# Issuing one group's load of x three bundles later in a fused convolution and channel-mix kernel

## The chip, the cores and the metric

The kernel runs on one core of one Trainium2 chip. The metric is the device time of one launch in microseconds. Before the change it is 434.34 us, the median of three runs (433.48, 434.34 and 434.85). The profile is of one further execution, with a span of 432.2 us.

The engines of a core are named as in the profile: PE is TensorE (PEld its weight loads), DVE is VectorE, ACT is ScalarE, POOL is GpSimd, SP is SyncE. SP and POOL start transfers here: SP those of the convolution's result and of the output, POOL those of x.

## The reference

There are 8 sequences of 4160 rows with 192 channels. The first half is a causal convolution over 7 rows, with 8 heads of 24 channels and softmaxed weights; the second half mixes each row with the one before it and sends it through a gated two-layer network.

```python
# weight: (8, 7), softmaxed over its last axis -> w
out = np.einsum('hk,bskhg->bshg', w, x_unf)     # 7 rows back, per head; called y below

x_prev = shift(y, 1)                            # the row before, zeros at the start
xk = mu_k * y + (1.0 - mu_k) * x_prev           # = x_prev + mu_k * (y - x_prev)
xr = mu_r * y + (1.0 - mu_r) * x_prev
k = np.maximum(xk @ w_k, 0.0)                   # 192 -> 1024
v = k * k @ w_v                                 # 1024 -> 192
r = 1.0 / (1.0 + np.exp(-(xr @ w_r)))
return (r * v).astype(np.float32)
```

(Shortened: `shift` stands for a concatenation with zeros.)

## The kernel before

The sequences are taken in four pairs. Work is cut into **steps** of 512 rows of a pair, and emitted in **bundles** of four k-slots; a full step has 8 slots, so two bundles. The first pair has steps of 256, 7 times 512 and 256 rows and fills bundles 0 to 15; the second pair's first step begins at bundle 16.

Ahead of the steps runs the convolution, in **groups** of up to ten blocks of 120 rows. There are six groups for the first pair (numbers 0 to 5) and four for each other pair (6 to 9 for the second, and so on). A group goes through these stages:

- `load_x`: POOL loads x for both sequences of the pair into a buffer `xb` of a ring of three, from f32 in memory to bf16 in the buffer. A full group is two transfers of 480 KB.
- `conv_half`, `conv_out`: PE multiplies `xb` with a banded matrix `toe`, in four units; ACT copies the result to `y`.
- `y_write`: SP writes `y` to memory (`y_dram`).
- `y_read`: SP reads it back transposed into `yT`, channels on partitions. (Groups 1 to 3 are transposed on PE instead, group 0 in a way of its own.)

A step then takes the difference of neighbouring rows from `yT` (`diff`), and makes xk and xr of it on DVE (`scale`, `add_y`). These feed the k and r matmuls.

```python
three = ctx.enter_context(tc.tile_pool(name="three", bufs=3))
...
def x_tile(g):
    p, blk0, nb, _, _ = groups[g]
    xb = three.tile([P, GB, 2, D], BF16, tag="xb", name="xb")
    xbs[g] = xb
    if g > 4:
        nc.vector.memset(xb[0:1, 0, 0, 0:2], 0.0)
    ...

def load_x(g):
    ...
    for s in range(2):
        ...
        nc.gpsimd.dma_start(out=xb[:, lo:hi, s, :], in_=bass.AP(...))   # the line that the profile calls L125

def y_write(g):
    ...
    nc.sync.dma_start(out=y_drams[p][blk0 * BLK : (blk0 + nb) * BLK, :]..., in_=ys[g][:BLK, :nb, :])

def y_read(g):
    ...
    nc.sync.dma_start_transpose(
        out=yTs[p][:, :, YC + r0 : YC + r1], in_=y_drams[p][r0:r1, :]
    )
```

When each stage is emitted is kept in tables by bundle. `fb` is the bundle of the first step that needs the group.

```python
for g, (p, blk0, nb, fb, on_pe) in enumerate(groups):
    ...
    elif p == 0:
        xs = {2: [0], 3: [1, 1], 4: [2, 2, 3, 3], 5: [4, 4, 5, 5]}[g]   # bundles of the conv units
    else:
        xs = range(fb - 10, fb - 10 + nx)
    ...
        at(late, xs[-1], y_write, g)
        at(late, xs[-1] + (1 if g < 6 else 2), y_read, g)
    if g > 3:
        b = {4: 1, 5: 1, 6: 2}.get(g)
        b = first_bundle[first_step[p]] + (-15, -11, -7, -3)[(g - 6) % 4] if b is None else b
        at(early, b, x_tile, g)
        at(early, b, load_x, g)
for s, (p, t0, L, n0, ns) in enumerate(steps):
    fb = first_bundle[s]
    ...
        if s == 4:
            at(mix_a, fb - 1, diff, s)
        else:
            at(mix_c, fb - 2, diff, s)
        at(mix_a, fb - 1, scale, s, 0, 0)
        at(mix_b, fb - 1, scale, s, 0, 1, 2)
        at(mix_b, fb - 1, scale, s, 1, 0)
        at(mix_c, fb - 1, add_y, s, 0)
```

For the groups that matter here this gives:

| group | rows of the pair | load issued in bundle | convolution in bundles | y_write | y_read | first needed by |
|---|---|---|---|---|---|---|
| 4 | 1920 to 3119 of pair 0 | 1 | 2, 2, 3, 3 | 3 | 4 | diff of step 4, in bundle 6 |
| 5 | 3120 to the end of pair 0 | 1 | 4, 4, 5, 5 | 5 | 6 | diff of step 6, in bundle 9 |
| 6 | 0 to 1199 of pair 1 | 2 | 6, 7, 8, 9 | 9 | 11 | first step of pair 1, bundle 16 |
| 7 | 1200 to 2399 of pair 1 | 16 - 11 = 5 | 10, 11, 12, 13 | 13 | 15 | third step of pair 1 |
| 8 | 2400 to 3599 of pair 1 | 16 - 7 = 9 | 14 to 17 | 17 | 19 | fifth step of pair 1 |

One bundle emits its work in this order, and each engine runs its own instructions in the order of emission:

```python
def bundle_rest(b, ns):
    units = xt.get(b, []) + [None, None]
    quad = vq.get(b, [None])[0]
    for n in bundles[b - 1][2:] if b > 1 else ():
        k_square(n)                      # DVE, the last two of the bundle before
    run(mix_a, b)
    k_mm(ns[0]); k_relu(ns[0]); k_square(ns[0])      # PE, ACT, DVE
    run(mix_b, b)
    conv_half(units[0], 0)
    k_mm(ns[1])
    conv_half(units[0], 1)
    k_relu(ns[1]); k_square(ns[1])
    run(rq, b)                           # the r matmuls
    run(first, b)
    if quad: v_rows(*quad, 0)            # 32 matmuls
    conv_half(units[1], 0)
    k_mm(ns[2])
    conv_half(units[1], 1)
    k_relu(ns[2])
    if quad: v_rows(*quad, 1)            # 32 matmuls
    run(mix_c, b)
    k_mm(ns[3]); k_relu(ns[3])
    if quad: v_out(*quad)                # product on DVE, two output stores of 192 KB on SP
    run(late, b)
```

`run(early, b)` comes before this. (Several calls are put on one line here.)

Of the kernel before, what the change touches and what calls it, by code (L numbers as in the profile page):

```python
# [14 lines left out]
def kernel(  # L15
# [254 lines left out]
    def conv_units(g):  # L270

        if groups[g][2] * 4 * G <= BANK:
            return [((0, 1), (6, 7)), ((2, 3), (4, 5))]
        return [((0,), (1,)), ((3,), (4,)), ((6,), (7,)), ((2,), (5,))]
# [367 lines left out]
    def at(table, b, fn, *a):  # L642
        table.setdefault(b, []).append((fn, a))
# [11 lines left out]
    for g, (p, blk0, nb, fb, on_pe) in enumerate(groups):  # L655
        nx = 1 if g < 3 else len(conv_units(g))
        if g == 0:
            continue
        if g == 1:
            xs = []  # L660
        elif p == 0:
            xs = {2: [0], 3: [1, 1], 4: [2, 2, 3, 3], 5: [4, 4, 5, 5]}[g]
        else:
            xs = range(fb - 10, fb - 10 + nx)
        for i, b in enumerate(xs):
            if g == 2:
                at(late, b, conv, g, i)
            else:
                xt.setdefault(b, []).append((g, i))
        if on_pe:  # L670
            for j in range((nb + 3) // 4):
                at(first, g - 1, tr, g, j)
        else:
            at(late, xs[-1], y_write, g)

            at(late, xs[-1] + (1 if g < 6 else 2), y_read, g)
        if g > 3:

            b = {4: 1, 5: 1, 6: 2}.get(g)
            b = first_bundle[first_step[p]] + (-15, -11, -7, -3)[(g - 6) % 4] if b is None else b  # L680
            at(early, b, x_tile, g)
            at(early, b, load_x, g)
# [174 lines left out]
```

## Time and profile before

| what | value |
|---|---|
| time, median of three | 434.34 us |
| span of the profiled execution | 432.2 us |
| PE busy | 411.6 us, 95% |
| DVE busy | 381.4 us, 88% |
| ACT busy | 347.5 us, 80% |
| POOL busy | 48.9 us, 11% |
| moved by the DMA engines | 64.58 MB, mean 149 GB/s |
| the chain that ended last | PE 88%, DMA 5%, DVE 3% |
| in that chain, DMA into yT | 4% |

A row of the profile's timeline gives start, length, engine, the line of the kernel, the operation with its destination and source, and the number of instructions. A bracket holds the time that the engine idled before, and the instruction or transfer that ended this. For a transfer, a row of SPq or POOL is its issue; when the data has landed is told apart from that. The chain of work that ended last is followed back from the last instruction, at each step to what released it: what is not in the chain can get faster without any effect on the end. The slices cut the span into 40 equal parts, with the busy share in tenths.

### The profile page before, as it was taken

Reading aid. Unit: us, or ns where it says so; the run is one execution under the profiler, and the core shown is the slowest. Engines: PE = TensorE matmul, PEld = TensorE weight load, DVE = VectorE, ACT = ScalarE, POOL = GpSimd, SP = SyncE. Lnnn points to the kernel's source line nnn. Section 1 sums busy time; section 2 is a strip of 40 time slices with the busy share of each in tenths; the row PEclk is TensorE's granted clock in tenths of the full one; section 3 lists DMA queues with packets and bytes.
Section 4 is the critical chain, followed back from the end, with each engine's and each line's share of the span. In section 5 each row is a group of like instructions: output and inputs, shape, how many; then the busy total and the mean of one; then the engine's idle time right before and its main releaser. Section 6 shows DMA issues by size and latency. Waiting matters only on the chain.

```text
span 432.2 us, 15786 instructions
## 1 busy us (share of the span) xinstructions
PE 411.6 (95%) x6845; PEld 315.7 (73%) x6845; DVE 381.4 (88%) x678; ACT 347.5 (80%) x407; POOL 48.9 (11%) x73
## 2 busy tenths in 40 slices
PE   7799974999999999999999999999999999999995
PEld 3456752777787887787777877787777877777795
DVE  5887827899999999999999999999999999999973
ACT  4878972889888898889888888889888888777771
POOL 6550100020203010020203010020200000000000
PEclk9989995999999999999999999999999999999999
DMA  8996795395949989395849999395848573411223
GB/s 133 192 180 95 178 188 164 83 215 136 183 119 192 208 170 202 87 212 145 172 131 169 227 172 197 83 212 148 176 125 149 160 162 118 109 56 64 74 77 110
DMA packets 134502, 64.58 MB, mean 149 GB/s; under 512 B 85132, under 2 KB 134048, under 8 KB 134432
## 3 DMA queue, kind: packets, MB, share of 16 engines
q1 hardware_dynamic: 96050, 48.31, 43.9%
q0 software_dynamic: 37488, 14.66, 29.8%
q8 instruction: 53, 0.87, 0.8%
q10 hardware_dynamic: 894, 0.61, 0.5%
q14 instruction: 17, 0.14, 0.1%
HBM read 29.92 MB, written 36.99 MB: 155 GB/s over the span
## 4 chain that ended last, share of the span: by engine, by line
PE 88%; DMA 5%; DVE 3%; ACT 1%; POOL 1%; issue 1%; SPq 0%; ACTq 0%; DVEq 0%
PE ps_k L490 38%; PE ps_v L592 37%; PE ps_r L564 7%; PE ps_c L291 5%; DMA yT<-y_dram 4%; DMA wk<-in_moe_w_k_dram 2%; PE ps_v L547 1%; DVE k L533 1%; ACT k_sb L519 1%; DVE d L433 0%; DVE xk L470 0%; DVE xk L464 0%; POOL xb L125 0%; PE ps_t L380 0%; DVE yT L389 0%
## 5 line engine op out<-in xcount | busy, mean ns | idle before, releaser
L519 ACT ACTIVATE k_sb<-ps_k 128x1024 bf16<-128x1024 f32 x260 | 260.9, 1037 | 63.9 <-PE ps_k L490 63.6
L490 PE MATMUL ps_k<-xk,wk 64*128 64x512 bf16 (+1 forms) x1632 | 203.4, 370 | 10.0 <-DVE xk L470 9.5
L533 DVE TENSOR_TENSOR k<-k_sb 128x1024 bf16<-128x1024 bf16 x260 | 177.6, 688 | 15.9 <-ACT k_sb L519 8.4
L592 PE MATMUL ps_v<-wv,k 64*128 64x192 bf16 x4032 | 188.8, 243 | 0.6 <-ACT k_sb L519 0.6
L592 PEld LDWEIGHTS <-k 64*128 64x128 bf16 x4032 | 172.3, 94 | 13.2 <-issue 0.6
L490 PEld LDWEIGHTS <-wk 64*128 64x128 bf16 x1632 | 87.5, 95 | 63.7 <-DVE xk L470 10.2
L608 DVE TENSOR_TENSOR o_sb<-ps_v,r_sb 128x768 f32<-128x768 f32 x64 | 61.2, 957 | 14.0 <-PE ps_v L592 9.8
L336 ACT CAST y<-ps_c 120x960 bf16<-120x960 f32 (+4 forms) x67 | 50.9, 787 | 6.4 <-PE ps_c L291 6.4
L572 ACT ACTIVATE r_sb<-ps_r 128x768 bf16<-128x768 f32 x65 | 54.6, 840 | 0.0
L125 POOL DMA_DIRECT2D xb<-in_x_dram x34 | 30.8, 911 | 208.0 <-PE ps_c L291 140.1
L564 PEld LDWEIGHTS <-xr 64*128 64x128 bf16 x780 | 36.1, 95 | 13.3 <-DVE xb L105 2.0
L564 PE MATMUL ps_r<-wr,xr 64*128 64x192 bf16 x780 | 44.0, 243 | 1.7 <-DVE xb L105 1.7
L291 PE MATMUL ps_c<-xb,toe 64*128 64x480 bf16 (+2 forms) x240 | 40.3, 343 | 0.0
L433 DVE TENSOR_TENSOR d<-yT 128x1536 bf16<-128x1536 bf16 (+2 forms) x35 | 31.0, 887 | 8.7 <-DMA yT<-y_dram 8.6
L464 DVE TENSOR_SCALAR xr<-d,mu 128x512 bf16<-128x512 bf16 (+1 forms) x102 | 35.1, 348 | 0.0
L464 DVE TENSOR_SCALAR xk<-d,mu 128x512 bf16<-128x512 bf16 (+1 forms) x99 | 32.8, 361 | 0.1
L470 DVE TENSOR_TENSOR xr<-xr,yT 128x1536 bf16<-128x1536 bf16 (+1 forms) x33 | 31.0, 939 | 1.1
L470 DVE TENSOR_TENSOR xk<-xk,yT 128x1536 bf16<-128x1536 bf16 (+1 forms) x32 | 30.2, 942 | 0.0
L291 PEld LDWEIGHTS <-toe 64*128 64x128 bf16 x240 | 13.5, 96 | 12.4 <-issue 1.1
L417 POOL COPY y_tail<-yT 128x195 bf16<-128x195 bf16 x4 | 1.8, 453 | 68.5 <-DMA yT<-y_dram 68.5
L719 PE MATMUL warm<-zeros,ones_t 128*128 128x512 bf16 x16 | 5.6, 530 | 1.8 <-DVE zeros L734 1.8
L107 POOL MEMSET xb<- 32x384 bf16 x3 | 1.2, 408 | 45.9 <-PE ps_k L490 43.7
(54 smaller groups left out, 64.3 us busy)
## 6 DMA issues: line engine op xcount, KB each, us to landing
out_dram<-o_sb SPq DMA_DIRECT2D x128, 192.0 KB, 2.7
y_dram<-y SPq DMA_DIRECT2D x10, 900.0 KB, 6.5
xb<-in_x_dram POOLq DMA_DIRECT2D x14, 480.0 KB, 8.2
xb<-in_x_dram POOLq DMA_DIRECT2D x6, 432.0 KB, 8.2
xb<-in_x_dram POOLq DMA_DIRECT2D x10, 192.0 KB, 5.2
y_dram<-y SPq DMA_DIRECT2D x3, 450.0 KB, 5.6
y_dram<-y SPq DMA_DIRECT2D x1, 810.0 KB, 6.7
xb<-in_x_dram POOLq DMA_DIRECT2D x2, 384.0 KB, 7.4
```

Of the source, the lines that this page charges most:

```text
L291: nc.tensor.matmul(out=banks[:, bank, :, :, k * G : (k + 1) * G], lhsT=toe[q, h, :], rhs=xbs[g][q, :nb, :, h * G : (h + 1) * G], start=hal ...
L336: copy(out=bass.AP(tensor=y.tensor, offset=y.offset + d0, ap=[y.ap[0], [d1 - d0, 2], [2 * D, nb], [Q, 2], [1, n]],), in_=bass.AP(tensor=ps ...
L433: nc.vector.tensor_tensor(out=shaped(s, diffs[s][:, cs, :L]), in0=y_of(s, cs, 1), in1=y_of(s, cs, 0), op=ALU.subtract)
L464: nc.vector.tensor_scalar(out=t[:, c, :L], in0=diffs[s][:, c, :L], scalar1=mu[:, i, c : c + 1], scalar2=None, op0=ALU.mult)
L470: nc.vector.tensor_tensor(out=o, in0=o, in1=y_of(s, sl, 0), op=ALU.add)
L490: nc.tensor.matmul(out=ps[:, i, f * L : (f + 1) * L], lhsT=wk[r, c, fs], rhs=xk[r, c, :L], start=c == 0 and f == 0, stop=c == NC - 1 and f ...
L519: nc.scalar.activation(out=k_sb, in_=ps.rearrange("p a b -> p (a b)"), func=AF.Relu)
L533: nc.vector.tensor_tensor(out=o, in0=i, in1=i, op=ALU.mult)
L564: nc.tensor.matmul(out=ps[:, i, k * D : (k + 1) * D], lhsT=xr[q, c, ts], rhs=wr[q, c, :], start=c == 0, stop=c == NC - 1,)
L572: nc.scalar.activation(out=r_sbs[s, j], in_=ps[:, :, 0 : 2 * D], func=AF.Sigmoid)
L592: nc.tensor.matmul(out=v_ps[s, j][:, bank, k * D : (k + 1) * D], lhsT=k2s[s][q, f, t * P : (t + 1) * P], rhs=wv[q, f, :], start=half == 0 ...
L608: nc.vector.tensor_tensor(out=o_sb.rearrange("p (b t) d -> p b (t d)", b=2), in0=v_ps.pop((s, j)), in1=r_sbs.pop((s, j)), op=ALU.mult,)
```

## The change

Only the bundle changes in which group 7's buffer is taken and its load is issued: 8 instead of 5. Its convolution stays in bundles 10 to 13. The change is meant to keep this load from running beside transfers of the first pair that are wanted sooner.

```diff
@@ -676,7 +676,7 @@
             at(late, xs[-1] + (1 if g < 6 else 2), y_read, g)
         if g > 3:
 
-            b = {4: 1, 5: 1, 6: 2}.get(g)
+            b = {4: 1, 5: 1, 6: 2, 7: 8}.get(g)
             b = first_bundle[first_step[p]] + (-15, -11, -7, -3)[(g - 6) % 4] if b is None else b
             at(early, b, x_tile, g)
             at(early, b, load_x, g)
```

## The prediction

> **What bounds the kernel now.** I read the page's slices first, then the chain of work that ended last, then the timeline around the one hole that the chain shows, then the same kind of transfer elsewhere in the trace. The slices (each 432.2 / 40 = 10.8 us):
>
> ```profile
> PE   7799974999999999999999999999999999999995
> ...
> PEclk9989995999999999999999999999999999999999
> ```
>
> TensorE is busy at nine tenths or more from slice 7 to slice 38, at the full clock. After the start-up there is one weak place: slices 5 and 6 (54 to 76 us), where PE falls to 7 and 4 tenths and its clock to half in slice 6. The chain of waits names it (start, length, what):
>
> ```profile
> 50.42 15.70 DMA yT<-y_dram
> 66.15 0.97 DVE d L433
> 70.42 1.46 PE ps_k L490 x6
> ```
>
> Everywhere after this the chain is PE work end to end. So for 15.7 us the end of the kernel hangs on one transposed read, the y_read of group 4 (the fifth group). The timeline shows what is issued beside it and who waits (start, length, engine, line, operation; in brackets the idle time before and its releaser):
>
> ```profile
> 49.97 1.88 POOL L125 DMA_DIRECT2D xb<-in_x_dram  x2 [19.57 <-PE ps_c L291]
> ...
> 50.42 10.82 SPq L367 DMA_TRANSPOSE yT<-y_dram  x1
> ...
> 57.79 1.50 PE L592 MATMUL ps_v<-wv,k 64*128 64x192 bf16 x32
> ...
> 61.07 0.83 PE L490 MATMUL ps_k<-xk,wk 64*128 64x512 bf16 x6
> ...
> 66.15 0.96 DVE L433 TENSOR_TENSOR d<-yT 128x1536 bf16<-128x1536 bf16 x1 [8.60 <-DMA yT<-y_dram]
> ...
> 70.42 1.46 PE L490 MATMUL ps_k<-xk,wk 64*128 64x512 bf16 x6 [8.52 <-DVE xk L470]
> ...
> 74.47 1.48 PE L592 MATMUL ps_v<-wv,k 64*128 64x192 bf16 x32
> ...
> 80.60 1.49 PE L592 MATMUL ps_v<-wv,k 64*128 64x192 bf16 x32
> ```
>
> The two POOL transfers are the x loads of group 7, the ones the change moves; they start 0.45 us before the transposed read. DVE stands still 8.60 us in front of diff(4), PE 8.52 us in front of the first k matmul of bundle 7, which needs the xk that follows from that diff. The 32-matmul rows (first half of the v product) mark the bundles: bundle 6 at 57.79, bundle 7 at 74.47, bundle 8 at 80.60. Bundle 7 to 8 takes 6.13 us; bundle 6 to 7, with the same set of work (one convolution unit, one quad), takes 16.68 us. **The excess is 16.68 - 6.13 = 10.55 us.** 8.52 of it is idle PE; the other 2.03 us is work at half clock after the pause (six k matmuls in 1.46 us against 0.83 at 61.07).
>
> Is the read slow because of the loads? I asked for windows (length, PE, PEld, DVE, ACT, POOL busy, clock, DMA share, GB/s), and for the landing of other y_reads:
>
> ```profile
> 58.00:62.00 4.00, 3.90 (x76) 3.00 (x70) 0.00 (x0) 3.20 (x5) 0.00 (x0) 1.00 1.53 131
> 62.00:66.10 4.10, 0.00 (x0) 0.00 (x0) 0.00 (x0) 0.96 (x1) 0.00 (x0) 0.74 1.18 298
> ```
>
> From 58 to 62 the DMA engines are full and move 131 GB/s. The x loads land 7.9 and 12.4 us after their issues at 49.97 and about 50.9, so the second lands at 63.3; after that the rate goes to 298. The packets recorded in the trace say the same for the transpose alone: its 3600 packets of 256 bytes go at some 280 per us while the x packets of 384 bytes flow beside them one for one, and at some 950 per us once those are through.
>
> ```profile
> 104.52 4.16 SPq L367 DMA_TRANSPOSE yT<-y_dram  x1
> ...
> 129.36 5.01 SPq L367 DMA_TRANSPOSE yT<-y_dram  x1
> ```
>
> These two are reads of the same size (ten blocks, groups 6 and 7) with no x load started beside them: issue takes 4.16 and 5.01 us against 10.82, and they land in 6.3 and 7.0 us against 15.7. The nine other ten-block reads of the trace land in 6.3, 7.0, 7.0, 7.5, 8.4, 6.8, 7.4, 7.4 and 6.7 us: median 7.0. Beside none of them does a load start at the same time; the next x load comes some 5.5 us after the read's issue, at its tail.
>
> **What the skill says.** The Trainium skill, "DMA: Bandwidth & Descriptors", section "Issuing engines are not separate DMA queues": transfers started by sync, scalar and gpsimd run on the same 16 DMA engines and interleave. Its section "Queues, rings and completion order" adds that each DMA engine goes round robin between the queues with work, packet by packet. The trace agrees: one-for-one packet counts, and the SP transpose crawling while the POOL load runs. The Trainium skill, "TensorE: Matmul & The Clock Gate", section "Part 1: The HAM clock gate": an idle window of about 3.4 us halves the array's clock. Here PE stops at 61.90 and the clock reads 0.50 from 65 to 74 us, so a pause of a microsecond should not bring this on; no run yet shows that.
>
> **The change part by part.** *Removed from bundle 5:* one 59 ns memset and two issues of 480 KB at 49.97. *Added at bundle 8:* the same. Nothing else changes in work or in order; the tile ring hands out buffers in the same order, since group 8's is still taken later, at bundle 9.
>
> *The transposed read.* It is issued at 50.42, when the y_write of group 4 (issued 43.72) has landed. That stays. Without the x load I take 7.0 us, the median of the nine, so it lands at 57.4. DVE reaches diff(4) after its two squares, which start at 56.03 and take 1.52: at 57.55. So DVE does not wait: the 8.60 us go, as long as the landing takes under 57.55 - 50.42 = 7.13 us.
>
> *From diff to PE.* From the start of diff(4) at 66.15 to the end of add_y of xk (69.41 + 0.95 = 70.36) DVE works 4.21 us without a gap. Started at 57.55 that ends at 61.76. PE is through with bundle 6 at 61.07 + 0.83 = 61.90. So the PE wait of 8.52 us goes too, but with a margin of only 0.14 us: every later microsecond is paid in full. Put the nine landings in: five are under 7.13 us and cost nothing, the others cost 0.37, 1.27, 0.27 and 0.27, on average over the nine 0.24. I allow 0.2 us.
>
> *The clock.* With no pause, the half-clock stretch goes, and its 2.03 us.
>
> *The load at its new place.* Bundle 8 would start some 6.1 us before group 8's memset at 85.00, so at 78.9 in the old time, 68.3 in the new (minus 10.55). First POOL issue about 69.2, second 70.1. The y_read of group 5 gets earlier too: its y_write no longer waits behind a 10.82 us issue (it stood at 62.47), goes out near 57.2, lands 6.7 us later at 63.9, and the read takes 5.3: 69.2. So load and read barely touch. With the landings of undisturbed pairs (6.3 and 7.9; 7.2 and 8.8; 7.8 and 10.1) group 7 is in the buffer at 78 to 80. Its first convolution stands at 91.31 in bundle 10, new time 80.8. The lead is enough by 1 to 3 us: cost 0, with a small risk.
>
> *Sum.* -8.52 - 2.03 + 0.2 = -10.35; 434.34 - 10.35 = **424.0 us**.
>
> **The rivals.** *1. The read is slow by itself,* being the first of its kind and right behind two output stores. Then nothing changes: 434. For it: it is the only slow one and the first. Against it: the rate goes up when the loads end, and later reads also follow two stores. *2. The wait only moves to group 7's convolution in bundle 10.* The lead falls from five bundles to two. If the load met the read of group 5 or group 8's load and took the 12.4 us it takes now, it would land at 82.5, 1.7 us late: 425.7. Against it: group 8's load starts a bundle later on the same queue, behind it. *3. DVE becomes the bound in bundle 6.* It has 0.14 us of slack; a read that takes 8.4 us, like the longest, costs 1.3: 425.3. *4. Half the gain:* the output stores ahead of the read hold it back to 60 us, PE waits 2.5 us without losing its clock: 426.5.
>
> **Range and chances.** Rival 1 gets about 3%, since the packets show the sharing. Rivals 2 and 3 spread the result upwards by 1 to 2 us; downwards there is little, as 10.55 us is all that this hole holds: 423.2 with luck in the run. Range 423.0 to 426.0. A gain over 2% needs 8.5 us (425.8 or less): 0.84. Within 2%: 0.15. Slower by over 2%: 0.01.
>
> **What would show it.** In the changed kernel's trace: the transposed read at 50.4 should have an issue of 4 to 5 us and land in about 7; the idle time of DVE before diff(4) and of PE before bundle 7 should each be under 0.5 us; the clock should stay at 9 in slices 5 and 6; bundle 6 to 7 should take 6.1 to 6.4 us; POOL should issue group 7's load near 69 us, and no PE wait on xb should stand in bundle 10. A read of still 10 us or more with no load beside it would prove me wrong, and so would a new PE pause near 81 us.

## The result and the profile after

| | before | after |
|---|---|---|
| time, median | 434.41 us (433.48 to 434.85, 4 runs) | 424.19 us (423.17 to 425.11, 4 runs) |
| ratio, 95% interval | 1 | 0.9767 (0.9738 to 0.9795) |
| span of the profiled execution | 432.2 us | 421.5 us |
| transposed read of group 4, issue to landing | 15.7 us | 7.6 us |
| DVE idle before diff(4) | 8.60 us | 0.45 us |
| PE idle before bundle 7's first k matmul | 8.52 us | 0.37 us |
| bundle 6 to bundle 7 | 16.68 us | 6.69 us |

The kernel is faster by 2.3%. The slices of the page after, for PE and its clock:

```profile
PE   6779999999999999999999999999999999999995
...
PEclk9999999999999999999999999999999999999998
```

Counted from 0, the dip of PE in slices 5 and 6 and the halved clock in slice 6 are gone. The chain of work that ended last, from the profile after (start, length, what):

```profile
49.62 7.55 DMA yT<-y_dram
...
57.19 0.97 DVE d L433
...
60.53 0.89 DVE xk L470
...
61.47 0.82 PE ps_k L490 x6
```

It still goes through the transposed read, diff and xk, so there is still no slack here; only the read's 15.70 us have become 7.55. The timeline after, around the same place and at the load's new one:

```profile
48.63 0.89 SPq L616 DMA_DIRECT2D out_dram<-o_sb  x2
...
49.62 4.00 SPq L367 DMA_TRANSPOSE yT<-y_dram  x1
...
56.98 1.50 PE L592 MATMUL ps_v<-wv,k 64*128 64x192 bf16 x32
57.19 0.96 DVE L433 TENSOR_TENSOR d<-yT 128x1536 bf16<-128x1536 bf16 x1 [0.45 <-DMA yT<-y_dram]
...
61.47 0.82 PE L490 MATMUL ps_k<-xk,wk 64*128 64x512 bf16 x6 [0.37 <-DVE xk L470]
...
63.67 1.50 PE L592 MATMUL ps_v<-wv,k 64*128 64x192 bf16 x32
...
68.08 0.06 DVE L105 MEMSET xb<- 1x1 uint32 x1
...
68.69 1.88 POOL L125 DMA_DIRECT2D xb<-in_x_dram  x2 [37.99 <-PE ps_c L291]
...
69.81 1.50 PE L592 MATMUL ps_v<-wv,k 64*128 64x192 bf16 x32
```

The issue of the read holds SP for 4.00 us and not 10.82. The rows of 32 v matmuls stand 63.67 - 56.98 = 6.69 us apart from bundle 6 to 7, and 69.81 - 63.67 = 6.14 from 7 to 8: of the excess of 10.55 us, 0.55 is left. Behind bundle 7 nothing has changed: from its row of v matmuls to the end it is 432.2 - 74.47 = 357.7 us before and 421.5 - 63.67 = 357.8 after.

Of the 10.7 us between the two spans, 16.68 - 6.69 = 9.99 lie in this one bundle. The other 0.8 lies ahead of it (the y_write of group 4 stands at 43.72 before and at 42.92 after), where the change touches nothing. The trace before has the clock at half from 23.0 to 26.4 us and the trace after has not: at 23 us the kernel before is still 0.3 us ahead, and from 33 us on it is 0.8 us behind. It is scatter of the start-up.

### The profile page after: what moved, and what is told of

Same layout as the page of the kernel before. It is cut to its first block, busy times and chain, and to the rows that moved or that the text cites. A ratio compares the mean times of both kernels' runs of the same rounds, so it can differ in the third digit from the quotient of the medians.

```text
span 421.5 us, 15786 instructions
## 1 busy us (share of the span) xinstructions
PE 408.0 (97%) x6845; PEld 314.5 (75%) x6845; DVE 380.8 (90%) x678; ACT 347.4 (82%) x407; POOL 48.9 (12%) x73
## 4 chain that ended last, share of the span: by engine, by line
PE 89%; DMA 6%; DVE 3%; ACT 1%; issue 0%; POOL 0%; SPq 0%; DVEq 0%; ACTq 0%
PE ps_v L592 38%; PE ps_k L490 38%; PE ps_r L564 7%; PE ps_c L291 4%; DMA xb<-in_x_dram 3%; DMA yT<-y_dram 2%; PE ps_v L547 1%; DMA w_raw<-in_weight_dram 1%; DVE d L433 0%; DVE k L533 0%; ACT k_sb L519 0%; ACT y L336 0%; DVE xk L446 0%; DVE o_sb L608 0%; POOL xb L125 0%
## 5 line engine op out<-in xcount | busy, mean ns | idle before, releaser
L490 PE MATMUL ps_k<-xk,wk 64*128 64x512 bf16 (+1 forms) x1632 | 200.9, 367 | 2.3 <-DVE xk L470 1.4
```

The costliest lines, as they stand in the source:

```text
L490: nc.tensor.matmul(out=ps[:, i, f * L : (f + 1) * L], lhsT=wk[r, c, fs], rhs=xk[r, c, :L], start=c == 0 and f == 0, stop=c == NC - 1 and f ...
```

## The experiments

Unless told otherwise, ratios are to the kernel before on the same chip, with their 95% intervals.

**1. Half of the load beside the read, moved by the order of emission alone.** The two sequences of group 7 are loaded apart (`load_x` takes the sequences as a further argument here).

```diff
+            if g == 7:
+                at(early, 5, x_tile, g)
+                at(early, 5, load_x, g, (0,))
+                at(early, 8, load_x, g, (1,))
+                continue
```

> Group 7's first sequence (480 KB) is loaded at bundle 5 as before the change, the second at bundle 8 as after it. Sharing by packets: the transposed read is held up for about half as long as before, so it lands in 11 to 12 us (15.7 before, 7.6 after), DVE waits about 4.5 us for it and PE about 4.3, with at most 2 us more if the clock drops: 428 to 430 us. Rival, a toll of fixed size for any load started beside the read: about 434 us. Rival, the read is slow by itself: no dependence on the half left, 424 us.

Measured: 434.80 us, ratio 1.0002 (0.9984 to 1.0021), no gain at all. This did not prove a toll of fixed size, as the timeline shows (POOL rows only, from 40 to 95 us):

```profile
50.05 1.88 POOL L125 DMA_DIRECT2D xb<-in_x_dram  x2 [19.30 <-PE ps_c L291]
86.20 1.89 POOL L125 DMA_DIRECT2D xb<-in_x_dram  x2 [34.28 <-PE ps_c L291]
```

Both transfers went out at 50.05, and the row at 86.20 is already group 8. The second one stands at bundle 8 in the order of emission, but POOL has nothing else to do between bundles 5 and 8 and nothing to wait for, so it ran ahead. What had held the load back so far is the memset of one element on DVE in `x_tile`: DVE comes to it in its own order, and the transfer has to wait for it. (The bracket names a matmul of the convolution instead. But before and after the change, and in experiments 3, 4 and 5, the issue comes 0.61 or 0.62 us after the start of the memset in L105, as 68.69 after 68.08 above, while the matmul ends anything from 0.06 to 0.35 us ahead of it.) The experiment had moved the emission without this gate, and was the kernel before over again.

**2. Half of the load, with the gate.** The edit is against experiment 1.

```diff
                 at(early, 5, load_x, g, (0,))
+                at(early, 8, lambda g: nc.vector.memset(xbs[g][0:1, 0, 1, 0:2], 0.0), g)
                 at(early, 8, load_x, g, (1,))
```

> As half_at_5, but with a one-element memset on VectorE into the second sequence's part of the buffer at bundle 8, so that POOL cannot run ahead with the second transfer. Sharing by packets: with 1280 packets of x beside it and not 2560, the transposed read lands in 10 to 11.5 us (15.7 before, 7.6 after); DVE waits 3 to 4.5 us for it, PE as long, and the clock may drop for a window: 427 to 429 us. Rival, a toll of fixed size for any load beside the read: 434 us. If the second transfer still goes out near 50 us, the memset is not what holds a load back.

Measured: 428.57 us, ratio 0.9865 (0.9833 to 0.9897). The timeline of this kernel:

```profile
49.46 0.94 POOL L125 DMA_DIRECT2D xb<-in_x_dram  x1 [18.46 <-PE ps_c L291]
...
49.91 8.10 SPq L367 DMA_TRANSPOSE yT<-y_dram  x1
...
61.32 0.96 DVE L433 TENSOR_TENSOR d<-yT 128x1536 bf16<-128x1536 bf16 x1 [4.27 <-DMA yT<-y_dram]
...
65.59 1.46 PE L490 MATMUL ps_k<-xk,wk 64*128 64x512 bf16 x6 [4.19 <-DVE xk L470]
...
74.69 0.06 DVE L684 MEMSET xb<- 1x1 uint32 x1
...
75.07 0.94 POOL L125 DMA_DIRECT2D xb<-in_x_dram  x1 [24.66 <-DVE xb L684]
```

Now the second transfer waits for the memset (L684) until 75.07. The read lands in 11.4 us. With none, half and the whole of the load beside it, the read takes 7.6, 11.4 and 15.7 us: steps of 3.8 and 4.3. (With the whole of the load beside it, it took 14.4 us in the trace of experiment 1 and 15.8 in both of experiment 7, so these steps are good to about 1 us.) The delay grows with the bytes, as packet sharing has it; a fixed toll is ruled out. The packet records show the sharing itself: from 54 to 55 us, 251 packets of x and 248 of the read started; from 57 to 58 us, with the load through, 3 and 876. In the changed kernel, with no load, 888 to 1132 packets of the read started in each microsecond from 52 to 55 us.

**3. Load one bundle earlier.** `7: 4` in place of `7: 8`.

> Group 7's load one bundle earlier than before the change, at bundle 4, where it starts beside the y_write of group 4 and not beside its y_read. Sharing by packets: the y_write lands 3 to 4 us later than its 6.7 us, and the y_read, which waits for it, starts late by as much: 427 to 430 us. Rival, only the transposed read suffers from a load: 424 us.

Measured: 432.71 us, ratio 0.9960 (0.9943 to 0.9977): slower than I expected by 3 us. The timeline:

```profile
43.64 1.88 POOL L125 DMA_DIRECT2D xb<-in_x_dram  x2 [12.87 <-PE ps_c L291]
...
44.09 0.50 SPq L359 DMA_DIRECT2D y_dram<-y  x1
...
52.33 9.88 SPq L367 DMA_TRANSPOSE yT<-y_dram  x1
...
64.22 0.96 DVE L433 TENSOR_TENSOR d<-yT 128x1536 bf16<-128x1536 bf16 x1 [6.30 <-DMA yT<-y_dram]
```

The y_write goes out at 44.09 and has landed, by the semaphore records (the times at which a transfer reports its parts done), 8.2 us later, against 6.4 us before and after the change; the read follows at once, at 52.33. That is the part I had expected, if smaller: 1.8 us more, and not 3 to 4. What I had not is that the load is slowed as well: its two transfers land 11.6 and 17.1 us after their issue, the second near 61.6. So it is still there when the read begins, and that takes 11.9 us. A load put ahead of the write hits both.

**4. Load at bundle 6 and at bundle 7.** `7: 6` and `7: 7`.

> Group 7's load at bundle 6, issued near 56 us, when the transposed read is about to land (57.2 after the change). Sharing by packets: the load's first packets come after the read's last, so nothing is lost: 424.2 us, within 0.7. Rival, the load has to stay away until bundle 8 (from the y_write and y_read of group 5 as well): over 426 us.

> Group 7's load at bundle 7, issued near 62 us, beside the y_write and y_read of group 5, which are wanted only at bundle 9. 424.2 us, within 0.7, like bundle 6 and bundle 8: the place between 6 and 8 does not matter. Rival, each bundle nearer to 8 helps: over 425 us.

Measured: 424.92 us, ratio 0.9766 (0.9729 to 0.9804), and 423.79 us, ratio 0.9740 (0.9696 to 0.9783). Both are where the change is, at 0.9767. Bundle 7 tells more (timeline):

```profile
64.08 1.88 POOL L125 DMA_DIRECT2D xb<-in_x_dram  x2 [33.27 <-PE ps_c L291]
64.53 8.04 SPq L367 DMA_TRANSPOSE yT<-y_dram  x1
```

Here the load meets the read of group 5 just as it had met that of group 4, and this read takes 14.5 us to land. It costs nothing, since its rows are wanted only at bundle 9. So the load does not have to wait for bundle 8; it only must not run beside the read of group 4, or beside the y_write ahead of it (experiment 3).

**5. Load at bundle 9.** `7: 9`.

> Group 7's load at bundle 9, issued near 75.3 us just ahead of group 8's. It lands 6.7 and 8.5 us after its two issues, at about 82 and 84.7, while its first convolution stands at 80.5. The lead is too short: PE waits about 4 us in bundle 10, perhaps 2 us more through the clock: 428 to 430 us. Rival, later is only better or harmless: 424 us.

Measured: 430.97 us, ratio 0.9909 (0.9875 to 0.9943). The timeline:

```profile
75.72 3.78 POOL L125 DMA_DIRECT2D xb<-in_x_dram  x4 [45.08 <-PE ps_c L291]
...
85.91 0.58 PE L291 MATMUL ps_c<-xb,toe 64*128 64x480 bf16 x2 [4.32 <-DMA xb<-in_x_dram]
```

The loads of groups 7 and 8 stand in one row. PE waits 4.32 us for group 7 in bundle 10, and its clock is halved for a while after this (granted 0.75 on average from 86 to 92 us). One bundle later than the change, two thirds of the gain are lost: 430.97 - 424.19 = 6.8 of 10.2 us.

**6. Another transposed read hit on purpose.** The changed kernel, with group 10's load a bundle earlier.

```diff
-            b = {4: 1, 5: 1, 6: 2, 7: 8}.get(g)
+            b = {4: 1, 5: 1, 6: 2, 7: 8, 10: 16}.get(g)
```

> The kernel after the change, with group 10's load moved from bundle 17 to 16, so that it starts beside the transposed read of group 7. Sharing by packets: this read, not the first of its kind, now lands in 14 to 16 us where it took 7.0; its data is wanted only some three bundles later, so the time stays at 424.2 us. Rival, only the first transposed read is slow: it still lands in 7 to 8 us. Rival, any slow read costs time: over 430 us.

Measured: 425.03 us, ratio 0.9756 (0.9710 to 0.9802). In the timeline the load's issues stand on both sides of the read's:

```profile
118.56 0.56 POOL L119 DMA_DIRECT2D xb<-in_x_dram  x1 [0.30 <-POOL xb L107]
118.73 5.46 SPq L367 DMA_TRANSPOSE yT<-y_dram  x1
119.11 1.02 POOL L125 DMA_DIRECT2D xb<-in_x_dram  x1
```

This read, the fourth in the kernel (of group 7), lands in 13.7 us where it took 7.0 in the kernel before. So it is not the first read that is slow, but the one with a load beside it. Nobody waits for it, and the time stays.

**7. Is the rest of the excess the clock?** The kernel before, with matmuls of zeros in PE's pause, first 30 and then 38.

```diff
         run(mix_a, b)
+        if b == 7:
+            warm(ring.tile([P, 2, BANK], FP32, tag="k", name="warm"), 30)   # then 38
         k_mm(ns[0])
```

> The kernel before the change, with 30 matmuls of zeros (128x128 by 512) at the head of bundle 7, in the pause of 8.52 us. They take about 6.5 us there, so PE stands still for no more than 2 us at a time. If 2.03 us of the excess are the halved clock after the pause, the clock stays at 9 tenths and the time falls by 2 us to about 432.3 although work is added. Rival, these 2 us are a backlog of DVE or ACT after the wait: no gain, 434.4 us or a little more.

> The filler of 30 matmuls ended 2.96 us before PE had work again, and the clock still fell to half for 3.4 us. With 38 they end near 69.6 us and leave under 1.5 us. If the halved clock is what makes the work after the pause slow, it stays at full in slices 5 and 6, and from the first k matmul of bundle 7 to its first row of v matmuls it takes 2.2 us, as after the change, and not 4.05 as before it: about 432.5 us. Rival, a backlog of DVE or ACT makes it slow: 3.6 us or more, and no gain in time, 434.5 us.

With 30: 433.12 us, ratio 0.9957 (0.9936 to 0.9978). The time fell as expected, but its trace did not bear out why: in the execution traced, of 433.98 us, a pause of 2.96 us was left, the clock went to half in it, and from the first k matmul of bundle 7 (70.80) to its v row (74.40) it still took 3.60 us. I take this one as inconclusive. With 38: 432.18 us, ratio 0.9954 (0.9936 to 0.9972). Timeline of the second:

```profile
61.12 8.38 PE L719 MATMUL warm<-zeros,ones_t 128*128 128x512 bf16 x38
...
66.37 0.96 DVE L433 TENSOR_TENSOR d<-yT 128x1536 bf16<-128x1536 bf16 x1 [9.53 <-DMA yT<-y_dram]
...
70.64 0.82 PE L490 MATMUL ps_k<-xk,wk 64*128 64x512 bf16 x6 [1.14 <-DVE xk L470]
...
73.05 1.50 PE L592 MATMUL ps_v<-wv,k 64*128 64x192 bf16 x32
```

Six k matmuls take 0.82 us where they took 1.46, the clock is at full throughout, and from the first k matmul to the v row it is 2.41 us: 4.05 before the change, 2.20 after it. DVE's wait is as long as ever (9.53 us). So some 1.6 to 1.9 us of the excess are the halved clock, and PE gets them back by being kept busy with nothing.

**8. The rest of the wait.** The changed kernel, with the y_write of group 4 put ahead of bundle 3's output stores, and diff(4) with its first scale behind the next square on DVE.

```diff
             if s == 4:
-                at(mix_a, fb - 1, diff, s)
+                at(mix_b, fb - 1, diff, s)
...
-            at(mix_a, fb - 1, scale, s, 0, 0)
+            at(mix_b if s == 4 else mix_a, fb - 1, scale, s, 0, 0)
...
+        if b == 3:
+            run(late, b)
         if quad:
             v_out(*quad)
-        run(late, b)
+        if b != 3:
+            run(late, b)
```

> The kernel after the change, with the y_write of group 4 ahead of bundle 3's output stores, and diff of step 4 after one square more. The read is issued about 1 us earlier; DVE's wait of 0.45 us before diff and PE's of 0.37 us at bundle 7 go. 423.8 us, 0.4 less than the changed kernel, which is inside the scatter of the times; the trace has to show it. Rival, the remaining wait is DVE's own work: unchanged waits.

> The changed kernel once more, to stand beside tuned_again on one chip: 424.2 us.

> The tuned kernel once more. By its trace PE's wait at bundle 7 was gone, worth 0.4 us: 423.8 us, if the changed kernel beside it has 424.2. The two intervals will overlap unless the gain is nearer to 1 us.

Measured: 423.23 us, ratio 0.9722 (0.9684 to 0.9760). Then both kernels side by side: the changed kernel 424.56 us, ratio 0.9774 (0.9747 to 0.9800), the tuned one 423.85 us, ratio 0.9760 (0.9735 to 0.9786). The medians differ by 0.7 us in the direction expected, and the intervals overlap, so the times do not show that it is better. The timeline of the second tuned run shows what became of the waits:

```profile
41.43 0.40 SPq L359 DMA_DIRECT2D y_dram<-y  x1
...
50.37 4.15 SPq L367 DMA_TRANSPOSE yT<-y_dram  x1
...
58.33 0.95 DVE L433 TENSOR_TENSOR d<-yT 128x1536 bf16<-128x1536 bf16 x1
...
61.02 1.79 PE L490 MATMUL ps_k<-xk,wk 64*128 64x512 bf16 x12
```

DVE and PE no longer wait (no brackets; PE goes through from bundle 6 to 7). This is due to the square put ahead of diff. The earlier y_write brought nothing: it goes out at 41.43, but the read still at 50.37, since on SP it stands behind bundle 4's output stores. Those issue right ahead of it in the changed kernel too (48.63 + 0.89, then 49.62). There the y_write has landed at 49.28 by the semaphore records, only 0.2 us before the stores are through at 49.52: write and stores hold the read back for nearly the same time, and to start it sooner both would have to be out of its way. Putting the read ahead of these stores was not tried.

## Why the prediction was right

The time came out at 424.19 us against 424.0. By its own steps:

- **The cause.** The read was slow because of the x load. Experiments 2 and 6 show it: delay in step with the bytes, and another read slowed in the same way. Rival 1 (slow by itself) falls with these and with the 7.6 us after the change.
- **The landing.** Expected 7.0 us, measured 7.55. The difference is inside the spread of the nine reads that I had taken it from (6.3 to 8.4).
- **From diff to PE.** I gave 0.14 us of slack and 0.2 us of cost. PE waited 0.37 us, for a DVE wait of 0.45: it is in fact paid nearly one for one. In the runs of bundles 6 and 7 the read landed 7.4 and 7.9 us after its issue; DVE waited 1.17 and 1.59 us and PE 1.09 and 1.51. The range had room for such waits, but most of this is not the landing; it is the next step.
- **Why the read starts when it does.** Here a step was wrong. I had it wait for the y_write to land. By the semaphore records that has landed at 50.11 before the change and at 49.28 after it; the read goes out 0.3 us later both times, behind the two output stores, with which SP is through at 50.33 and 49.52. In these two traces that hardly matters. In the runs of bundles 6 and 7 the same stores occupy SP for 1.73 us instead of 0.89, and the read goes out at 50.58 and 50.56, although the y_write has landed by 49.6. This is rival 4 in small. Why the second store then takes longer to issue stays open.
- **The clock.** Expected 2.03 us, and 1.6 to 1.9 by the filler. That short pauses keep the clock was left open in the prediction: the runs with 0.37, 1.14, 1.09 and 1.51 us of pause kept it, those with 2.96 and more lost it. The prediction took from the Trainium skill, "TensorE: Matmul & The Clock Gate", section "Part 1: The HAM clock gate", that an idle window of about 3.4 us halves the clock. Here less was enough: before the change the clock falls at 63.96 by its records, 2.06 us after PE stopped at 61.90, and with the filler of 30 a pause of 2.96 us did it. That the window runs freely, as the section also says, agrees with the traces (last part).
- **The load at its new place.** Issued at 68.69 and about 69.6 (expected 69.2 and 70.1), landed by 78.1 at the latest, and wanted at 80.53: 2.4 us to spare, of the 1 to 3 expected (1.0 in the second trace of the changed kernel, where it landed at 79.83 and was wanted at 80.84). Experiment 5 shows the edge one bundle further.
- **The price of being late.** Rival 2 was given 1.7 us for a load that comes 1.7 us late. The mechanism is real, but for a longer wait the price was too small: at bundle 9, 4.32 us of waiting cost 6.8 us. The 3.41 us at half the clock that follow add some 1.7 (an estimate: half of their length), and in that run the read of group 4 went out only at 50.42 and left PE waiting 1.33 us at bundle 7.
- **The sum.** Expected -10.35 us; -9.99 in the bundle by the traces, -10.2 by the medians. That the time was met within 0.2 us is partly luck: the start-up alone scattered by 0.8 us between the two traces, and the four runs after the change lie between 423.17 and 425.11.

What I had not seen is how the load is held to its bundle at all. The prediction moved "one memset and two issues" as if the issues would stay where they were emitted. They do so only for the memset.

## What to carry to other kernels

A transfer with time to spare can lengthen one that is wanted at once, here a read by about 4 us for each 480 KB beside it: look for loads that start together with a read on the critical chain, and move the load into the stretch between that read's landing and its own first use, here any of bundles 6 to 8. Place it with something that really holds it, since POOL, with nothing else to do, ran ahead of the order in which the code was written. And count a pause of TensorE of some 3 us or more as longer than it is, because slow matmuls followed each one here.

## What was not expected of the hardware

- The time for which the clock is halved goes in steps. By the clock records of the traces it was 3.41 us after pauses of 2.96 and 4.32 us, 6.83 us after 4.19 and 5.71 us, and 10.24 us after 8.52 us: one, two and three times 3.41. In every trace all changes of the clock lie a whole number of 3.41 us apart.
- What counted in such a stretch of 3.41 us was how long PE was busy in it; it did not have to stand still throughout. The clock fell at the end of stretches with 0.00 us of busy PE (bundle 9), 1.00 (filler of 30), 1.35 (before the change), 1.59 (bundle 4) and 1.70 (start-up before the change). It held after 2.37 (filler of 38) and 2.44 (bundle 7), and in the start-up of other runs after 1.7 and 1.9. In these traces the line is thus near half of the stretch.
- The sharing works both ways, and can slow the load more than what it meets: beside the y_write, the output stores and then the read, the second transfer of the load in experiment 3 took 17.1 us, against 8.5 and 9.9 us in the two traces of the changed kernel.
- The slowed read also holds the engine that issues it: the issue occupied SP for 4.00 us with no load beside it, 8.10 with half and 10.82 with the whole. (For the slowed reads of experiments 4 and 6 it was 8.04 and 5.46 us, so it does not follow the landing in step.) Output stores behind it have to wait for this long.
